# A fused attention and two-mixer kernel: another order for the first 500 steps, and another tile layout and rounding order in the last stage

## The chip, the cores and the metric

The kernel runs on one core of a Trainium2 chip. The metric is the device time of one execution in microseconds. The core has five engines that each run their own instructions in order: TensorE (PE in the profile, with PEld for its weight loads), VectorE (DVE), ScalarE (ACT), GpSimd (POOL) and SyncE (SP), which here only issues DMAs.

## What is computed

Three layers follow one another on 4 batches of 576 rows with 512 channels: attention (a pooled one and one over a band of 7 keys, added), a token mixer and channel mixer, and a second mixer that multiplies by cosine and sine. The weights come as 64-bit floats.

```python
a_d   = sm_attn(mean4(q), mean4(k), mean4(v))        # 8 heads, 144 pooled rows
a_loc = softmax over |i - j| < 4 of q k^T / 8, times v
x = repeat(a_d, 4) + a_loc                            # (4, 576, 512)
u = x + (relu(x^T @ w_tok1) @ w_tok2)^T
x = u + relu(u @ w_ch1) @ w_ch2
theta = x @ w_theta
y = w_tok_r @ (x cos(theta)) + w_tok_i @ (x sin(theta))
u = x + y
out = u + relu(u @ w_ch)
```

## The kernel before

Each matrix product is done with operands split into a rounded part and a rest (`split`, L150: a cast on ScalarE, a subtraction on VectorE), in three matmuls (`mm3`, L155).

**The front.** Everything up to the last stage is written as generators, one for each step; the string ORDER lists in which order they are advanced, one entry for one call (`G3` is one call, `I*2` two). Each call issues the instructions up to the generator's next yield, and every engine then runs what it was issued in exactly that order. Whatever stands first in the list stands first in each engine's queue, and a waiting instruction holds up all that is listed behind it on its engine. The steps of the first 500 entries:

- `P` (16) loads the q and k of a pair of heads (582 KB, 4 buffers); `K` pools them on VectorE (two additions). `W` loads the values of a pair for the band, in 4 DMAs. `V` (8, one for each group of two pairs) loads pooled values (650 KB, one buffer) and adds them on GpSimd in two additions and a product.
- `L` is the band attention of a pair, 8 calls: TensorE starts the scores (with 24 or 12 warming matmuls for the first four pairs, WARM), scores (80 matmuls), VectorE maximum and difference, ScalarE exp, TensorE transposes, ScalarE copies, TensorE output (80 matmuls), VectorE normalization.
- `F` is the pooled attention of a group Q, 9 calls; the seventh normalizes on VectorE, the eighth stores the result (`od`), the ninth waits for that store and loads it back repeated (`xu`). `A` adds `xu` to a pair on VectorE.
- `T` is the token mixer of a group: T.1 casts x on ScalarE, T.2 subtracts on VectorE (`xl`, L606), T.3 copies rows on ScalarE, T.4 and T.5 are the first product on TensorE, T.6 to T.9 the second. `E` evicts and splits the hidden rows, `U` evicts the output (ScalarE twice) and stores it to `uT` from a tile with one buffer.
- `C` is the first part of the channel mixer for 384 columns: C.1 loads from `uT` (so it waits for the stores of `U`), C.2 casts, C.3 subtracts, C.4 to C.11 are TensorE's. `H` and `O` evict.
- `G0` to `G6` and `X` convert 64-bit weights (`converted`): a DMA, a pair of instructions on ScalarE, three on VectorE (L203, L206, L215), one on GpSimd, a cast on ScalarE, a subtraction on VectorE. G0 and G1 are 512 KB, G2 128 KB, G3 to G6 288 KB each, X0 to X7 512 KB each. X28 to X31 are early parts of a late weight; they load through the GpSimd queue (X29 through SP) and write the halves back to memory. X30 is a small one of 64 columns.

A number behind a dot after these names is the call: T2.4 is the fourth call of group 2's T. Steps such as E2.1 carry a dot in their names already; they are told apart by the text.

**The last stage** (from L1333) is ordered by a scheduler, not by hand. For each batch `stage_z` (L1160) makes theta on TensorE in chunks, turns it to cosine and sine, multiplies by x and splits into zh and zl; chunk (4, 1) holds the last 64 rows of two batches, which go to the small tiles eh and el. Batch 0 does this in two halves of 256 columns. `stage_y` (L1202) multiplies by the token weights, reading eh/el first, then zh/zl. The tiles z, uh and ul come from one pool that lies where the front's last tiles were, and a first write to a tile waits until the tile that lay there before has been read.

Of the kernel before, what the change touches and what calls it, by code (L numbers as in the profile page):

```python
# [43 lines left out]
C0 V6 V5 L8 X3 E3.1 L9 H0.3 F5 E3.1 X3 W10 L9 F6 X3 F5 L10 V6 A9 T3 F5 T3 V6 U3.0 L10 K14 T3 V6 U3.0 X6 U3.0 T3 H0.3
X3 X6 X29 X31 X30 X28 L11*2 C0 L11 P15 U3.1*2 A8 F6 U3.1 C0 F5 T4 X29*2 X28*2 X30*2 L11 L12 L10 O0.1 K15 C0 C1 W11 L10
X29 O0.0 X28 C0 T4 X28 T4 F7 O0.3 O0.2 L12 C1 O0.3 T4 L12 F7 L12 T4 C1 L11 E4.1 F6 L11 F7 L11 F6 C1 A10 W12 E4.0 L11
X28 X30*2 X28 X29*3 F6 F7 E4.0 A11 X30*2 F7 X28*3 L12 E4.1 C1 H1.0 T5 C2 F6 L13*2 H1.1 X31 X30 X29 L12 H1.1 T4 T5 T4
U4.0 L13 X30 X29 X30 X29 C1 U4.0 H1.0 U4.0 L13 V7 T4 H1.2 T5 L13 L15 L13 X31*5 T4 U4.1 X31 L12 U4.1 L15 L12 X31 W15 V7
C1 H1.2 A12 V7 U4.1 T5 H1.3 V7 X31 H1.3 L13 E5.0 C1 L13 F7 C1 F7 E5.0 F7 L15 L14*2 A13 L15 C1 O1.0 L14 F7 O1.1 L14 T5
W14 C1 E5.1 C2 E5.1 T6 L14 L15 L14 T5 T6 T5 U5.0 C2 T5 U5.0 L15 U5.0 T5 O1.2 T6 O1.3*2 L15 L14 T6 U5.1 L14 U5.1*2 L15  # L50
T6 E6.0 A14 A15 C2 E6.1 C3 E6.0 T7 E6.1 T6 T7 H2.0 T6 U6.0 H2.0 T7*2 U6.0*2 C3 T6*2 T7 U6.1*2 E7.0 U6.1 C2 E7.1*2 E7.0
T7 H2.1*2 T7 U7.0 T7 U7.0*2 T7 C2*2 H2.2 U7.1 H2.2 U7.1 C3 U7.1 R0 X8 X17 H2.3 X11 H2.3 C2 X19 C2*2 X8 O2.1 X8 C2 O2.2
X8 O2.0 X11 C3 O2.3*2 X21 C3 H3.0 X19 H3.0 X19 X8 C3 X17 X8 X17 C4 H3.1 C3 H3.2*2 X17 H3.1 X19 X20 H3.3 X21 H3.3 C3
X11 X9 C3 C4 O3.0 X21 X17 X19 C3 C4 X21 C3 O3.2 X11 X21 X13 C4 O3.3 O3.1 X21 O3.3 X12 X17 X9 C4 X9 X20 X19 C4 X9 H4.0
X13 H4.0 X20 C5 C4 X15 H4.2 H4.1 X9 H4.1 X20 H4.2 H4.3 B2 X16 H4.3 C4 X9 X13 C4 C5 X13 X20 C4 O4.1 X12 X10 C5 X13 C4
O4.2 X12 B2 C5 O4.0 X12 X11 X13 C5 O4.3 H5.0 X20 X16 O4.3 X23 B2 C5 H5.1 X10 H5.0 X10 C5 H5.2 X12 X11 X10 H5.1 B2 H5.3
X14 X10 H5.3 J2 H5.2 X16 C5 M2.4 X23 X10 X16 X23 X15 C5 X18 C5 O5.1 X23 X22 B2 O5.2 O5.0 X12 X15 X14 C5 X23 X14 X16
M2.5 B2 O5.3 X14 X16 O5.3 R1 X18 X15 X23 X32 X33 M2.4 X34 M2.5 X35 X22 X18 X14 B2 X15 X22 X18 M2.6 B2 X18 X14 X22 M2.7
X15 X18 X22 B2 M2.6 M2.8 X22 M2.7 B2 M2.8 M2.9*2 B2 M2.10*2 B3 M2.11*2 S0 S1 S2 S3 S4 B2 S5 S8 S6 S9 S7 B2 S10 S11 B3
S12 S13 N2.0 S14 B3 S15 B2 S16 S17 S18 S19 S20 N2.1 S21 S22 S23 S24 S25 N2.0 B2 S26 N2.0 S27 S28 N2.2 S29 S30 S31 S32  # L60
N2.1 S33 N2.1 S34 S35 B3 S36 S37 S40 N2.3 S41 S38 S39 B3 M3.4 N2.2 S42 N2.2 S43 S44 B3 S45 S46 N2.3 S47 M3.5 S48 N2.3
S49 S50 B3 M3.6 S51 M3.4 S52 N2.3 S53 M3.5 S54 S55 B3 M3.7 S56 S57 S58 M3.6 M3.7 B3 M3.8 S59 S60 M3.8 S61 S62 J3 S63
B3 M3.9 R3 PL0 X32 M3.9 PL0*2 X33 B3 X32 M3.10 X34 X33 X32 M3.11 X32 M3.10 X33 M3.11 X35 X32 B3 X34 X32 PS0 B3 X33
N3.0 X34 PT0.0 N3.0 PT0.0 PS0 N3.0 X34 B3 PT0.0 PS0 PT0.1 N3.1 PT0.1*2 B3 PT0.3 N3.2 PT0.3 N3.1 PT0.3 N3.1 PT0.2
PP0.0.1 PS0 PT0.2 PP0.1.1 PT0.2 PP0.0.3 N3.3 PH0.0.1 N3.2 PP0.1.3 PH0.1.1 N3.3 N3.2 PP0.0.2 X33 X35 PP0.1.2 PH0.0.2
N3.3 PP0.0.5 PH0.1.2 PH0.0.2 X35 PP0.1.5 N3.3 PH0.0.5 X33 PH0.0.5 PP0.0.6 X35 PH0.1.5 PP0.1.6 PH0.1.5 PH0.0.6 PP0.2.1
PH0.1.6 PH0.0.6 X34 PH0.0.6 X34 X35 X24 PH0.1.2 X35 PP0.3.1 PH0.1.6*2 PP0.0.7 PP0.1.7 PH0.0.7*2 PP0.0.4 PH0.1.7
PH0.0.7 X24 PP0.1.4 PH0.0.4 PP0.2.3 PH0.1.7 PH0.1.4 PH0.0.4 X24 PH0.2.1 PP0.3.3 PH0.3.1 PH0.1.4 PP0.2.2 PH0.1.7 X24
PH0.0.4 PP0.3.2 PH0.2.2 PH0.1.4 X24 PH0.2.2 PP0.2.5 PH0.3.2 PP0.3.5 PH0.2.5*2 PP0.2.6 PH0.3.5 PP0.3.6 PH0.3.5 PH0.2.6
PH0.3.6 PH0.2.6 PP0.2.7 X24 PH0.3.6 PP0.3.7 PH0.2.7 X25 PH0.2.7 PP0.2.4 PH0.3.7 PH0.2.6 PH0.3.7 PP0.3.4 PH0.3.6  # L70
PH0.2.7 J1 PH0.3.7 X27 PH0.3.2 X41 X25 PL1 PH0.2.4 PL1 PH0.3.4 PL1 PH0.2.4 X25 PH0.3.4 D1*2 PH0.2.4 X25 N1.0 PH0.3.4
X25 N1.0 X27 N1.0 X25 X27 X41 D1 X26 N1.1 X27 X41 PS1 X27 N1.1 D1 X41 N1.2 N1.1 PT1.0 X41 N1.2 X27 N1.2 X41 X26 N1.3
X41 PT1.0 X26 PT1.0 X26 D0 N1.3 PT1.1 X26 N1.3 D0 X26 PT1.1 J0 PT1.1 N1.3 PT1.3 PS1 PT1.3 D0 PT1.3 PS1 N0.0 N0.1 N0.0
# [1361 lines left out]
```

## Time and profile before

| | us |
|---|---|
| median of 3 timed runs | 686.59 |
| lowest, highest | 684.61, 690.44 |
| the profiled execution | 681.57 |
| its span, first to last instruction | 679.80 |
| TensorE busy | 655.9 |
| VectorE busy | 521.0 |
| ScalarE busy | 321.2 |
| GpSimd busy | 98.5 |

The busy times are shares of one profiled execution. The time of a step list is best read by stretches: what an engine did between two moments, and what ended its idle time.

### The profile page before, as it was taken

What the parts mean: (1) busy time and instruction counts of PE and PEld (TensorE: products, weight loads), DVE (VectorE), ACT (ScalarE), POOL (GpSimd) and SP (SyncE); (2) the same over time, 40 slices, a digit from 0 to 9 for tenths busy, and PEclk for the clock granted to TensorE, in tenths of its full rate; (3) what the DMA queues carried; (4) which work ended last, traced back from release to release, by engine and by line L of the source; (5) the groups of instructions that cost most, each with busy time, mean ns of one, the idle gap of its engine ahead of it and who ended that gap; (6) DMA issues with size and microseconds to landing.
All of it is one profiled execution on the core that took longest, in us unless ns stands there. A gap on an engine that the chain in (4) does not pass through costs nothing.

```text
span 679.8 us, 17390 instructions
## 1 busy us (share of the span) xinstructions
PE 655.9 (96%) x7320; PEld 626.7 (92%) x7320; DVE 521.0 (77%) x952; ACT 321.2 (47%) x632; POOL 98.5 (14%) x92
## 2 busy tenths in 40 slices
PE   6769899999999999999999999999999999999997
...
GB/s 282 239 277 229 250 274 260 252 179 238 110 157 104 242 293 186 202 62 207 66 194 127 209 142 85 238 324 279 130 63 0 112 114 1 62 141 1 71 1 69
DMA packets 93022, 109.93 MB, mean 162 GB/s; under 512 B 46881, under 2 KB 69537, under 8 KB 92945
## 3 DMA queue, kind: packets, MB, share of 16 engines
...
## 4 chain that ended last, share of the span: by engine, by line
PE 84%; DVE 8%; DMA 3%; ACT 3%; SPq 1%; issue 1%; DVEq 0%; ACTq 0%
PE y L157 6%; PE y L158 6%; PE y L159 6%; PE c L157 4%; PE c L158 4%; PE c L159 4%; PE c L699 4%; PE c L702 4%; PE c L700 4%; PE c_p L905 3%; PE c_p L902 3%; PE c_p L903 3%; PE t L157 2%; PE t L159 2%; PE t L158 2%; DMA qk<-qkT 2%
## 5 line engine op out<-in xcount | busy, mean ns | idle before, releaser
L157 PE MATMUL y<-wrh,zh 128*128 128x288 f32 x256 | 75.0, 296 | 0.8 <-ACT zh L151 0.8
L158 PE MATMUL y<-wrl,zh 128*128 128x288 f32 x256 | 74.9, 296 | 0.0
L159 PE MATMUL y<-wrh,zl 128*128 128x288 f32 x256 | 72.9, 295 | 0.0
L219 POOL TENSOR_TENSOR ww<-ww,raw 128x512 int32<-128x512 int32 (+2 forms) x30 | 41.1, 1373 | 159.2 <-DMA raw<-w_ch 52.5
L157 PEld LDWEIGHTS y<-wrh,zh 128*128 128x128 f32 x256 | 48.0, 188 | 1.1 <-ACT zh L151 1.1
L158 PEld LDWEIGHTS y<-wrl,zh 128*128 128x128 f32 x256 | 48.0, 188 | 0.0
L159 PEld LDWEIGHTS y<-wrh,zl 128*128 128x128 f32 x256 | 47.3, 188 | 0.0
L219 POOL TENSOR_TENSOR raw<-raw 128x512 int32<-128x512 int32 (+2 forms) x16 | 20.0, 1249 | 136.7 <-DVE raw L215 74.1
L1212 DVE TENSOR_TENSOR cx<-y,cx 128x288 f32<-128x288 f32 x32 | 14.4, 455 | 30.3 <-PE y L159 29.9
L151 ACT CAST cuh<-cx 128x288 fp32r<-128x288 f32 (+1 forms) x16 | 8.8, 553 | 57.5 <-DVE cx L1212 57.4
L157 PE MATMUL th<-thh,cxh 128*128 128x512 f32 (+1 forms) x92 | 31.6, 343 | 0.0
L158 PE MATMUL th<-thl,cxh 128*128 128x512 f32 (+1 forms) x92 | 31.6, 343 | 0.0
L159 PE MATMUL th<-thh,cxl 128*128 128x512 f32 (+1 forms) x92 | 31.6, 343 | 0.0
L199 ACT ACTIVATE ww<-raw 128x512 f32<-128x512 f32 (+2 forms) x30 | 19.5, 649 | 25.3 <-DVE c1l L223 9.4
L921 DVE SCALAR_TENSOR_TENSOR g<-c,g 128x384 fp32r<-128x384 f32 x40 | 21.1, 550 | 12.9 <-ACT g L918 12.9
L918 ACT ACTIVATE g<-c 128x384 fp32r<-128x384 f32 x40 | 19.1, 490 | 24.4 <-PE c L159 24.3
L201 ACT ACTIVATE raw<-raw 128x512 int32<-128x512 uint32 (+3 forms) x46 | 29.5, 640 | 0.0
L568 PE MATMUL o<-vw,plt 38*32 38x65 f32 x1280 | 18.0, 236 | 6.9 <-issue 3.6
L929 DVE TENSOR_TENSOR ut<-c,ut 128x384 f32<-128x384 f32 x32 | 17.1, 551 | 9.8 <-PE c L702 9.8
L568 PEld LDWEIGHTS o<-vw,plt 38*32 38x32 f32 x1280 | 15.4, 110 | 9.6 <-issue 4.8
L157 PE MATMUL t<-w2h,h 128*128 128x256 f32 (+1 forms) x64 | 21.6, 337 | 0.0
L157 PE MATMUL c<-uh,c1h 128*128 128x384 f32 x64 | 21.4, 334 | 0.0
...
## 6 DMA issues: line engine op xcount, KB each, us to landing
...
```

The lines of the kernel that those rows point to most:

```text
L157: pe.matmul(out, lh, rh, start=start, stop=False, skip_group_check=again)
L158: pe.matmul(out, lh, rl, start=False, stop=False, skip_group_check=again)
L159: pe.matmul(out, ll, rh, start=False, stop=stop, skip_group_check=again)
L201: act.activation(f, words[:, :, 0], AF.Copy, scale=2.0**-29)
L219: pool.tensor_tensor(out=w.bitcast(I32), in0=w.bitcast(I32), in1=f, op=ALU.add)
L568: pe.matmul(o[r : r + 32, 5 * j + i // 2], pts[h : h + W, i // 2, r : r + 32], vw[h : h + W, g, :], start=True, stop=True,)
L699: pe.matmul(ps[:, 0:MIX], h[:, cb % 2, d], h1, start=cb == cbs[0], stop=False)
L700: pe.matmul(ps[:, 0:MIX], l[:, cb % 2, d], h1, start=False, stop=False)
L702: pe.matmul(ps[:, 0:MIX], weight[cb // 2][2][:, cb % 2, d], h2, start=False, stop=cb == cbs[-1])
L902: pe.matmul(ps[:, 0:MIX], h[:, cb % 2, d], h1, start=cb == cbs[0], stop=False)
L903: pe.matmul(ps[:, 0:MIX], l[:, cb % 2, d], h1, start=False, stop=False)
L921: dve.scalar_tensor_tensor(out=h2, in0=ps, scalar=0.0, in1=h1.bitcast(F32), op0=ALU.max, op1=ALU.subtract)
```

## The change

Two parts. First, the first 500 entries of ORDER are put in another order; they hold the same steps, the same number of times, and from entry 501 on the list is the same. Second, in the last stage the tile uh of batch 0 is allocated ahead of z (so it lies in front of z in the pool), the last rows of a pair's second batch are multiplied and rounded behind the next chunk's casts where the columns come in halves, and ordering edges put the first instructions of later chunks (the scaled copy of theta for the second half, the Abs of a next chunk) behind earlier casts on ScalarE.

```diff
 ORDER = """
-G3 P0 G2 I*2 P1 G3 P4 G3 V0 P2 G3 K0 G3 G2 I G2 I L0*2 P3 K1 F0 W1 L0 F0 L1 L0 G3 F0 V0 L1*2 P5 V0 L2 W0 G2 K2 V0 G2
-F0 G1 L1 V1 F0 L2 K3 G0 G6 K4 L0 F0 L0 L2 L1 G2 F1 L2 K5 L1 L0 F1 G1*2 F1 F0 V1 W3 L0 F1 G5 G0 L1 F0 G0 F1 G6 F2 L1 G0
-P6 W2 G5 G6 L3 V1 F2 F0 V1 L3 G6 F2 F1 L3 G1 G4 F1 L2 P7 L5 L2 K6 L5 F1 G1 L3 A0 V2 X0 A1 L3 G1 T0 L5 G0 T0 L2 G2 F1
-L3 G0 G4 F2 G5 T0*2 V2 X2 L2 G6 W5 F2 K7 V2 L4*2 E0.0*2 T0 L4 V3 V2 A2 L3 E0.1 L5 G4 L4 W4 L5 G6 L5 G4 L3 X2 F3 G5 P8
-P9 A3 G4 F2 G5 E0.1 T1 G4 G5 T0 F2 V3 L4 F3 F2 T0 L4 V3 X2 F3 L6 V3 L6 X7 T0 P11 L6 X2 X0 F3 K8 U0.0 L6 T0 X2 X0 U0.0
-F3 L4 U0.0 V4 K9 F2 F3 X0 L6 L4 L6 T1 F4 U0.1 X0 F3 T1 L5 U0.1 X0 T1 U0.1 F4 X7 X4 V4 F3 T1 X7 F4 W6 L5 X7 E1.1 F4
-E1.0 E1.1 L8 V4 L8 X7 E1.0 X1 A4 F4 T1 P10 A5 T1 X2 T2 L8 T1 U1.0*2 T2 T1 U1.0 X1 F3 L7 X7 L7 T2 X1 T2 X4 X5 K10 X1 L8
...
+P0 K0 G5 I*2 P1 I G1 V0 G6 L1 G4 K1 G1 L0 G3 G5 L1 G5 G1 P2 L0 L1 G2 P4 L0 G6 L0 G4 F0 G6 L2 V0 P3 G2 F0 G5 K2 L2 G2
+F0 L0 L2 V0 G3 F0 K3 L0 V1 X30 V0 F1 P5 G3 G2 G5 F1 W0 F0 V1 L2 L1 G2 L1 G4 K4 G0 L1 G6 F1 F0 X30 V1 W1 L0 P8 G4 G6 G0
+L0 F1 L3 F0 F1 K5 V2 G0 G1 L3*2 L1 G2*2 L1 L2 G1 F0 L2 X2 F0 G0 F2*2 L3 W2 L5 K8 X30 A1 A0 G6 X0 G5 L5 G3 F2 V2 L3 G3
+T0 G0 V1 F1 L5 X30 L3 F2 G4 P11 X0 G1 G3 P6 G0 X30 W3 X2 L4 F1 L4 T0 F2 K6 X0 X4 X2 L2 V2 V3 L2 T0 V2 X0 T0*2 X2 L4 L3
+X0 X2 E0.1 L4*2 P7 K7 W5 F1 L4 E0.0 V3 F2 E0.1 F3 X7 L3 L5 E0.0 L6 F3 F2 T0 G4 L6 F1 W4 L6 X30 P9 T0 F3 X1 U0.0 L5 F3
+L5 T0 V3 F2 X2 X7 L6 A2 U0.0 L4 A3 V4 T1 X7 T0 K9 F3 L6 U0.0 L6 X0 X1 T1 L4 V3 F3 T1 L5 X1*2 I T1 L5 L8 U0.1 E1.0 U0.1
+F2 L8 W6 X1 T1 E1.0 E1.1 F4 L8 L7*2 F3 F4 E1.1 A5 T1*2 U0.1 F4 T1 A4 X7 U1.0 P10 V4 F3 W7 L6 L7 U1.0 F3 U1.0 K10 X7 T1
+T2 L7 X1 L7*2 T2 X3 L8 V4 T2*2 K11 L7 U1.1*2 L6 E2.0 F4 E2.0 A6 F4 X4*3 T2 E2.1 L8 E2.1 L8 L7 P12 T2 A7 L9 X7 F5 U1.1
...
+U3.1 T4 U3.1 C1 X29 L10 L12 K15 C0 F7 X29 T4*2 X29 W11 F7 F5 F7 T4 L10 C0 L12 L13 C1 X29 O0.3 V6 X28 E4.0 O0.2 L12 F6
...
+    def behind(inst):
+        return tc.issue_after(inst.ins) if inst is not None else nullcontext()
...
-            act.activation(t[:, 0:n], ps[:, 0:n], AF.Copy, scale=1.0 / TWO_PI)
+            with behind(first):
+                act.activation(t[:, 0:n], ps[:, 0:n], AF.Copy, scale=1.0 / TWO_PI)
...
-            act.activation(g[:, 0:n], f[:, 0:n], AF.Abs)
+            with behind(first if per == 1 else cast):
+                act.activation(g[:, 0:n], f[:, 0:n], AF.Abs)
...
+                    cast = split(zh[:, i + b0 : i + b0 + nb, d], zl[:, i + b0 : i + b0 + nb, d], wv)
+                if rows:
+                    with behind(cast):
+                        last_rows(1, *rows)
+                    rows = ()
+                if b0 == 0:
+                    zcast = cast
...
+                rows = t[:, 0:width], g, f, xv
+                last_rows(0, *rows)
+                if per == 1:
+                    last_rows(1, *rows)
+                    rows = ()
+        return zcast
...
+    uh = rounded(0)
     z = new_z(0)
-    stage_z(0, 0, 256, *xhl, xx[1], *z)
-    stage_z(0, 256, DM, *xhl, xx[1], *z)
+    zcast = stage_z(0, 0, 256, *xhl, xx[1], *z)
+    stage_z(0, 256, DM, *xhl, xx[1], *z, first=zcast)
```

## Rows read from the trace of the kernel before

**Rows 1.** The page: span, and TensorE's busy tenths in 40 equal slices.

```profile
span 679.8 us, 17390 instructions
...
PE   6769899999999999999999999999999999999997
```

**Rows 2.** Stretches: busy PE, PEld, DVE, ACT, POOL (count); clock, DMA share, GB/s.

```profile
0.00:84.80 84.80, 67.20 (x1881) 54.03 (x1882) 70.67 (x135) 49.08 (x118) 26.81 (x31) 0.92 0.81 255
84.80:154.82 70.02, 68.80 (x1631) 62.24 (x1629) 60.21 (x112) 42.10 (x97) 18.00 (x17) 1.00 0.74 243
154.82:480.53 325.71, 325.65 (x2474) 322.96 (x2467) 243.49 (x436) 145.05 (x270) 53.65 (x44) 1.00 0.59 184
...
0.00:12.70 12.70, 7.95 (x151) 4.96 (x152) 6.47 (x15) 4.01 (x8) 2.57 (x8) 1.00 0.86 307
12.70:46.85 34.15, 24.81 (x856) 19.06 (x853) 28.40 (x55) 19.64 (x50) 9.56 (x10) 0.88 0.82 248
```

**Rows 3.** TensorE in time order: start, us, line, out<-in, shapes, count [idle before <-releaser].

```profile
86.43 0.39 PE L157 MATMUL t<-xh,w1h 128*128 128x256 f32 x1
...
154.82 0.44 PE L629 MATMUL t<-fixed,x 128*128 128x128 f32 x2
...
481.38 0.41 PE L157 MATMUL y<-wrh,zh 128*128 128x288 f32 x1 [0.84 <-ACT zh L151]
```

**Rows 4.** VectorE in order of time, 83 to 95 us.

```profile
83.32 1.48 DVE L606 TENSOR_TENSOR xl<-x,xh 128x1280 fp32r<-128x1280 f32 x1
...
85.57 0.43 DVE L203 TENSOR_SCALAR ww<-ww 128x512 f32<-128x512 f32 x1 [0.17 <-ACT ww L199]
...
89.84 0.56 DVE L546 TENSOR_TENSOR pbuf<-s,mx 128x380 f32<-128x380 f32 x1
...
93.68 0.68 DVE L223 TENSOR_TENSOR c10l<-ww,c10h 128x512 fp32r<-128x512 f32 x1
```

**Rows 5.** VectorE in order of time, 4 to 48 us.

```profile
4.23 0.31 DVE L206 TENSOR_SCALAR raw<-raw 128x288 uint32<-128x288 uint32 x1
...
9.71 0.76 DVE L421 TENSOR_TENSOR qa<-qk 128x576 f32<-128x576 f32 x1 [1.51 <-DMA qk<-qkT]
...
28.10 0.49 DVE L507 TENSOR_TENSOR ods<-od,rd 128x320 f32<-128x320 f32 x1
...
42.15 1.56 DVE L595 TENSOR_TENSOR x<-x,xu 128x640 f32<-128x640 f32 x2 [1.94 <-DMA xu<-ot]
...
47.71 1.33 DVE L206 TENSOR_SCALAR ww<-ww 128x288 uint32<-128x288 uint32 x1
```

**Rows 6.** GpSimd in order of time, 12 to 48 us.

```profile
12.79 1.34 POOL L398 TENSOR_TENSOR vd<-vd 128x650 f32<-128x650 f32 x1 [6.82 <-DMA vd<-vtok]
...
47.46 1.41 POOL L398 TENSOR_TENSOR vd<-vd 128x650 f32<-128x650 f32 x1 [10.48 <-DMA vd<-vtok]
```

**Rows 7.** ScalarE in order of time, three stretches.

```profile
24.05 0.66 ACT L199 ACTIVATE raw<-raw 128x512 f32<-128x512 f32 x1 [0.65 <-DMA raw<-w_tok]
24.61 0.64 ACT L201 ACTIVATE raw<-raw 128x512 int32<-128x512 uint32 x1
...
142.72 1.48 ACT L679 CAST uh<-ut 128x1536 fp32r<-128x1536 f32 x1 [0.47 <-DMA ut<-uT]
...
480.72 0.61 ACT L151 CAST zh<-tg 128x512 fp32r<-128x512 f32 x1
```

**Rows 8.** SyncE's DMA issues in time order: start and length of the issue.

```profile
29.93 0.61 SPq L510 DMA_DIRECT2D od<-ods  x1
...
34.15 0.61 SPq L516 DMA_DIRECT2D xu<-od  x1
...
131.51 0.33 SPq L656 DMA_DIRECT2D uT<-us  x1
...
132.61 1.21 SPq L519 DMA_DIRECT2D xu<-ot  x2
137.37 0.38 SPq L672 DMA_DIRECT2D ut<-uT  x1
```

More of the change, by code (lines that the diff above doesn't have):

```diff
@@ L1 @@
 import math
-from contextlib import ExitStack
+from contextlib import ExitStack, nullcontext
 from functools import partial
@@ L44 @@
[L44 to L73, printed above, removed]
@@ new lines @@
+F2 L8 W6 X1 T1 E1.0 E1.1 F4 L8 L7*2 F3 F4 E1.1 A5 T1*2 U0.1 F4 T1 A4 X7 U1.0 P10 V4 F3 W7 L6 L7 U1.0 F3 U1.0 K10 X7 T1
+T2 L7 X1 L7*2 T2 X3 L8 V4 T2*2 K11 L7 U1.1*2 L6 E2.0 F4 E2.0 A6 F4 X4*3 T2 E2.1 L8 E2.1 L8 L7 P12 T2 A7 L9 X7 F5 U1.1
+L9 X3 L9 V5 U2.0 T2 X3 X29 X4 V4 U2.0 L9 F5 C0*2 F4 X3 F5 P15 C0 W9 L10 T3 X5 T3 L10 V5 T2 W8 T2 U2.0 L9*2 C0 P13 L10
+L8 U2.1*2 X4 L8 H0.0 X5*2 H0.0 L10 L11*2 F4 C0 H0.1 X5 F4 X6 T3 H0.1 T3 L9 E3.0 X28 L11 X3 T3 E3.0 L10 X5 K12 X5 L10
+X6 L9 K13 E3.1 C0 X3 C0 V5 L11 H0.2 F5 X28*2 U2.1 V5 H0.3 X6 E3.1 X6 T3 F5 X28 X30 H0.3 X6 T3 H0.2 X30 V6 U3.0 L11 F6
@@ new lines @@
+P14 F6 T3 V6 L11 X6 U3.0 F5 X28 W10 F4 L12*2 F5 U3.0 A8 A9 F6 C0 T3 V6 F6 K14 X31 F5 L12 C0 O0.0 W12 U3.1 X28 F6 O0.1
+U3.1 T4 U3.1 C1 X29 L10 L12 K15 C0 F7 X29 T4*2 X29 W11 F7 F5 F7 T4 L10 C0 L12 L13 C1 X29 O0.3 V6 X28 E4.0 O0.2 L12 F6
+X28 C1 A10 F6 E4.0 T4 O0.3 L11 C1 L11 X28 F6 A11 C2 C1 H1.1 T5 E4.1 X29 H1.0 H1.1 E4.1 F7 X29 F7 X31 X29 X28 W13 F6
+L13 T4 T5 T4 U4.0 L13 X30 X29 X30 X29 C1 U4.0 H1.0 U4.0 L13 V7 T4 H1.2 T5 L13 L15 L13 X31*5 T4 U4.1 X31 L12 U4.1 L15
+L12 X31 W15 V7 C1 H1.2 A12 V7 U4.1 T5 H1.3 V7 X31 H1.3 L13 E5.0 C1 L13 F7 C1 F7 E5.0 F7 L15 L14*2 A13 L15 C1 O1.0 L14
@@ new lines @@
+PT0.3 N3.1 PT0.2 PP0.0.1 PS0 PT0.2 PP0.1.1 PT0.2 PP0.0.3 N3.3 PH0.0.1 N3.2 PP0.1.3 PH0.1.1 N3.3 N3.2 PP0.0.2 X33 X35
+PP0.1.2 PH0.0.2 N3.3 PP0.0.5 PH0.1.2 PH0.0.2 X35 PP0.1.5 N3.3 PH0.0.5 X33 PH0.0.5 PP0.0.6 X35 PH0.1.5 PP0.1.6 PH0.1.5
+PH0.0.6 PP0.2.1 PH0.1.6 PH0.0.6 X34 PH0.0.6 X34 X35 X24 PH0.1.2 X35 PP0.3.1 PH0.1.6*2 PP0.0.7 PP0.1.7 PH0.0.7*2
+PP0.0.4 PH0.1.7 PH0.0.7 X24 PP0.1.4 PH0.0.4 PP0.2.3 PH0.1.7 PH0.1.4 PH0.0.4 X24 PH0.2.1 PP0.3.3 PH0.3.1 PH0.1.4
+PP0.2.2 PH0.1.7 X24 PH0.0.4 PP0.3.2 PH0.2.2 PH0.1.4 X24 PH0.2.2 PP0.2.5 PH0.3.2 PP0.3.5 PH0.2.5*2 PP0.2.6 PH0.3.5
@@ new lines @@
+PP0.3.6 PH0.3.5 PH0.2.6 PH0.3.6 PH0.2.6 PP0.2.7 X24 PH0.3.6 PP0.3.7 PH0.2.7 X25 PH0.2.7 PP0.2.4 PH0.3.7 PH0.2.6
+PH0.3.7 PP0.3.4 PH0.3.6 PH0.2.7 J1 PH0.3.7 X27 PH0.3.2 X41 X25 PL1 PH0.2.4 PL1 PH0.3.4 PL1 PH0.2.4 X25 PH0.3.4 D1*2
+PH0.2.4 X25 N1.0 PH0.3.4 X25 N1.0 X27 N1.0 X25 X27 X41 D1 X26 N1.1 X27 X41 PS1 X27 N1.1 D1 X41 N1.2 N1.1 PT1.0 X41
+N1.2 X27 N1.2 X41 X26 N1.3 X41 PT1.0 X26 PT1.0 X26 D0 N1.3 PT1.1 X26 N1.3 D0 X26 PT1.1 J0 PT1.1 N1.3 PT1.3 PS1 PT1.3
+D0 PT1.3 PS1 N0.0 N0.1 N0.0 PT1.2 D0 N0.0 N0.2 PT1.2 PS1 N0.1 PT1.2 N0.1 PP1.0.1 N0.3 N0.2 PP1.1.1 PH1.0.1 N0.2
@@ L84 @@
+PH1.3.7 PP1.3.4 PH1.3.6 PH1.2.7 J4 PH1.3.7 PH1.3.2 J5 PH1.2.4 PH1.3.4 PH1.2.4 PH1.3.4 PH1.2.4 D4 PH1.3.4 R5 Z D4 N4.0
+X36 X37 N4.0 LR*2 N4.0 D4 N4.1 X38 LR N4.1 LR D4 N4.2 N4.1 X36*2 X43 X37 X44 N4.3 R6 X36 LR ZS X37 LR X36 N4.2 X37 X38
+ZS D5 N4.2 X36 ZS D5 N5.0 X37 LR ZS LR N5.0 ZS X37 ZS N4.3 ZS D5 N4.3 X43 ZS N5.1 X44 X38 N4.3 LR*2 N5.1 X38 D5 N5.2
+X43 X38*2 X43 X44 X43 N5.3 X44 X43 R6 Z N5.2 X44 N5.3 X44 N5.3*2 LC*2 N5.0 N5.1 N5.2
 """.split()
```

44 lines of the change are left out of this document (26 added, 18 removed).

## Prediction

> **What bounds the kernel now.** I read the page first, then the busy times by stage, then the waits and the order of single instructions on each engine. The page gives a span of 679.8 us and a TensorE that is hardly ever idle after the first slices [rows 1]. The stages make that sharp [rows 2]: in the first 84.80 us TensorE is busy for 67.20 us, so 17.6 us are lost; from 84.80 to 154.82 only 1.22 us are lost; from 154.82 to 480.53 0.06 us; then one gap of 0.84 us [rows 3]. The cut at 84.80 is where VectorE ends T2.2 (83.32 + 1.48) [rows 4]; T2.4, whose second matmul reads that result, starts on TensorE at 86.43, and T4.6, the first step behind the reordered part, at 154.82 [rows 3]. So behind T2.4 there is next to nothing to win, and the front is judged by one question: when does VectorE end T2.2 in the new order? VectorE is busy for 70.67 of the 84.80 us before it [rows 2].
>
> I map steps to rows by counting: every step issues a known number of instructions on each engine, in the order of the list, so the n-th instruction of an engine belongs to a known step.
>
> **The front, part one: VectorE up to T2.2.** The new list holds the same steps, so no instruction is saved. In front of T2.2 it puts everything that the old one had there, and more: X1.3, K10.1, L7.3 (these run from 85.57 to 90.40 in the old order, 4.83 us), X1.6 (0.68) and three small instructions of X30 (64 columns; the 288-column one took 0.31 [rows 5], so 0.6 for the three, 0.9 at most) [rows 4]. Together +6.1 us. What pays for it must be idle time.
>
> Start. The old order feeds VectorE early with G3, the smallest useful weight. The new one loads P0, G5, the constants, P1, G1, V0, and on ScalarE G1's pair of conversions stands in front of G5's, so VectorE, after K0 and K1, waits for G1. When does G1 land? In the old order P1 was there at 9.71 with 1693 KB queued up to it [rows 5], V0 at 12.79 with 2925 KB [rows 6]: 400 KB/us. In the new order 2077 KB are queued up to G1: about 10.7. G1's ScalarE pair costs 0.66 + 0.64 [rows 7] and G5's shorter one about 0.8, so VectorE starts G5.3 at about 12.7, having done only K0 and K1 (2.7 us): 10.0 us idle. The old order had by then 12.70 - 6.47 = 6.2 us idle [rows 2]. Term: +3.8 (between +3.0 and +4.6, by 0.8 us of G1's landing).
>
> Weight conversions beside GpSimd. G5.3 took 2.58 us in the old order, from 47.38 to 49.95; its second instruction took 1.33 where the same one took 0.31 at 4.23 [rows 5], and GpSimd was adding values at 47.46 for 1.41 [rows 6]. G1.3 (2.56, against 1.54 for its shape elsewhere) and G6.3 (2.0 against 1.08) show the same. In the new order these three run early. Free of GpSimd they would save 3.4 us, beside it nothing. V0 lands within a microsecond of them, so GpSimd's additions meet part of them: I take half, -1.7. [...]
>
> Waits between 12.70 and 46.85. VectorE was idle for 34.15 - 28.40 = 5.75 us there [rows 2]: 1.94 for the pooled rows xu [rows 5], the other 3.8 mostly short waits for TensorE. In the new order VectorE runs later against TensorE, so I keep 2.2 of the 3.8 (1.0 to 3.8). The xu trip: F0.7 ended at 28.59 and A0 started at 42.15, 13.6 us later [rows 5], of which SP spent time on other loads: od was issued 1.3 us after F0.7, xu 4.2 us after od, and landed 8.0 us after its issue [rows 8]. In the new order SP is free when F0.7 ends (about 33), so the trip should be some 10 us, and about 8.2 us of VectorE work lies between F0.7 and A1.1: a wait of 1.5 (0 to 5.4). Term: (2.2 + 1.5) - 5.75 = -2.05.
>
> Sum for T2.2: 84.80 + 6.1 + 3.8 - 1.7 - 2.05 = 91.0.
>
> **The front, part two: TensorE behind T2.2.** The TensorE work in front of T2.4 differs by three short steps of opposite sign (L6.7 and L7.5 ahead, F4.4 behind), which I set to nothing. If T2.4 starts later than 86.43, the 1.22 us of idle time behind it can go, so break-even is 86.43 + 1.22 = 87.65. At 91.0 the front costs 3.3 us. TensorE has no slack behind it [rows 2], so this reaches the end in full. C0, the next thing that TensorE needs from others, is not later than that: U1.1 is ready on ScalarE 1.6 us after T2.2, its store and C0's load cost together at most what they cost for C1 (5.9 + 5.4 [rows 7, 8]), the cast and the subtraction 1.5 and 1.8, in sum 16.2 behind T2.2; TensorE's own work from T2.4 to C0.4 is about 16.
>
> The clock: the granted clock averaged 0.88 from 12.70 to 46.85 [rows 2], so a part of that stretch ran at the lower level. I expect the same in the new order and charge nothing, because VectorE is the bound there.
>
> **The last stage.** TensorE waits once, 0.84 us at 481.38, for ScalarE's first rounded z, which ScalarE issues at 480.72 [rows 3, 7] although its input was ready some 5 us earlier. With u's tile in front, z no longer lies on the tile that is still being stored, and the new ordering puts the first casts ahead of the next chunk's Abs. The casts are not new, only earlier: 0.6 us each on a ScalarE that idles between. Deferred are the second batch's last rows, which batch 1 reads a whole stage later. Term: -0.85; bounds -0.85 and +0.5 (the second half's evictions now stand behind a cast, and if that cast waits for its memory, they wait too).
>
> **Sum.** +3.3 - 0.85 = +2.45 us: a profiled span of 682.2 instead of 679.8 (that execution took 681.57, below all three timed runs). Against the median of 686.59 this is 689.0.
>
> **Rivals.** (1) Slower: xu comes late. X2's load (512 KB) is now issued between od and xu; if the trip is the old 13.6 us and that load's 2.0 us (at 261 GB/s over that stretch) on top, A1 waits 7.4 instead of 1.5 us and everything up to T2.2 follows: 694.9. It decides as soon as xu lands behind about 41. For it: xu took 8.0 us from issue to landing. Against it: SP and its queue are emptier at that point. (2) Slower: a wait for a store. In the new list C1's load stands directly behind the store U3.1.3; in the old one SP waited from 133.8 to 137.37 for it, 5.9 us after the store's issue, with other work in between [rows 8]. Behind C1 now stand W11 and F5.9 (xu for A10 and A11), behind these on VectorE and ScalarE A10, A11, T5.1 and E4.1, and T4.6 needs E4.1: 5.9 + 0.4 + 1.7 + 8.0 + about 7 = 23 us from the store to T4.6, while TensorE has 440 matmuls in between, at 42 ns each [rows 2] 18.6 us, and is not yet through the step before. A wait of about 2.5 us: 691.5. (3) The start is better than I think: if the three conversions meet no GpSimd work and the short waits vanish, T2.2 ends at 86.6 to 87 and the front costs nothing or gains 1: 685 to 686.5. [...] (4) Faster by over 1%: T2.2 would have to end near 81.6; VectorE's own work in front of it is 70.67 + 6.1 = 76.8, which leaves 4.8 us of idle time where the start alone costs 10. (5) The last stage does not do what it says and its gap stays: 689.9.
>
> **Chances.** Forecast (T2.2 between 89 and 93, gap gone) 0.45; rival 1 0.13; rival 2 0.15; rival 3 0.20; rival 4 0.04; rival 5 0.03. The three runs shown spread over 684.61 to 690.44, so some 3 us either way come on top. The range reaches from rival 3 with a low run to rival 2 with a high one: 683.0 to 694.5; the likeliest case by itself spans 686 to 691.5. A measurement of this kernel tells about 1% (6.9 us) from no change; slower by more needs rival 1, or rival 2 with a high run: 0.14. Faster by more: 0.06. Same: 0.80.
>
> **What would show it.** Right: VectorE ends T2.2 (the third xl subtraction) near 91 instead of 84.80; its idle time before 12.7 is about 10 us; TensorE's T2.4 starts right behind it and T4.6 near 158; no wait of y for zh. Wrong: T2.2 before 87 (then rival 3), a wait of x for xu longer than 5 us (rival 1), TensorE waiting for h in front of T4.6 (rival 2), or TensorE idle for more than 2 us between 155 and 660.

## The result

| | before | after |
|---|---|---|
| median of 6 timed runs each, us | 684.39 | 692.67 |
| lowest, highest | 681.13, 690.44 | 690.84, 695.47 |
| span of the profiled execution | 679.8 | 691.5 |
| T4.6 starts on TensorE | 154.82 | 167.81 |
| from T4.6 to the end of the span | 524.98 | 523.7 |

The changed kernel is slower: the ratio is 1.0125, with a 95% interval of 1.009 to 1.016. The median of 692.67 lies inside the predicted range of 683.0 to 694.5, but the forecast was 689.0, so the loss was forecast at 2.45 us and is 8.3 us in the medians (11.7 in the two profiled spans). The front loses 13.0 us up to T4.6 (3.3 were forecast), and the stretch behind it gives 1.3 back. That the median lies in the range is luck: the range reached so far up for rival 2 with a high run, and rival 2 did not happen. A loss of over 6.9 us needed rival 1 or 2 in the prediction, which gave it 0.14; neither happened, and it came all the same.

### The profile page after: what moved, and what is told of

Same layout as the page of the kernel before. It is cut to its first block, busy times and chain, and to the rows that moved or that the text cites. A ratio compares the mean times of both kernels' runs of the same rounds, so it can differ in the third digit from the quotient of the medians.

```text
span 691.5 us, 17395 instructions
## 1 busy us (share of the span) xinstructions
PE 662.2 (96%) x7320; PEld 630.6 (91%) x7320; DVE 519.2 (75%) x952; ACT 320.3 (46%) x632; POOL 97.6 (14%) x92
## 4 chain that ended last, share of the span: by engine, by line
PE 89%; DVE 4%; DMA 3%; issue 1%; ACT 1%; SPq 1%; DVEq 0%
PE y L158 6%; PE y L157 6%; PE y L159 6%; PE c L699 4%; PE c L157 4%; PE c L702 4%; PE c L700 4%; PE c L159 4%; PE c L158 4%; PE c_p L905 3%; PE c_p L902 3%; PE c_p L903 3%; PE th L158 2%; PE th L159 2%; PE th L157 2%; PE t L157 2%
## 5 line engine op out<-in xcount | busy, mean ns | idle before, releaser
L921 DVE SCALAR_TENSOR_TENSOR g<-c,g 128x384 fp32r<-128x384 f32 x40 | 21.0, 549 | 17.1 <-ACT g L918 17.1
L929 DVE TENSOR_TENSOR ut<-c,ut 128x384 f32<-128x384 f32 x32 | 17.1, 550 | 10.2 <-PE c L702 10.2
L159 PE MATMUL c<-uh,c1l 128*128 128x384 f32 x64 | 21.4, 334 | 0.0
L158 PE MATMUL c<-ul,c1h 128*128 128x384 f32 x64 | 21.4, 334 | 0.0
```

What stands on the lines that cost most here:

```text
L158: pe.matmul(out, lh, rl, start=False, stop=False, skip_group_check=again)
L159: pe.matmul(out, ll, rh, start=False, stop=stop, skip_group_check=again)
L921: dve.scalar_tensor_tensor(out=h2, in0=ps, scalar=0.0, in1=h1.bitcast(F32), op0=ALU.max, op1=ALU.subtract)
```

## The profile after

First the stretches, which answer [rows 2]: how long, busy time (instructions) of PE, PEld, DVE, ACT and POOL, granted clock, DMA share, GB/s.

```profile
0.00:92.50 92.50, 72.85 (x2031) 57.35 (x2031) 74.22 (x146) 50.19 (x122) 28.81 (x33) 0.89 0.77 249
92.25:167.81 75.56, 70.22 (x1482) 63.04 (x1480) 55.49 (x103) 41.26 (x95) 16.95 (x19) 0.95 0.70 209
...
0.00:11.88 11.88, 8.68 (x200) 5.76 (x200) 2.49 (x5) 3.20 (x6) 1.76 (x7) 1.00 0.86 303
11.88:45.87 33.99, 21.26 (x657) 15.32 (x657) 29.49 (x59) 18.51 (x53) 15.45 (x15) 0.84 0.78 246
14.80:21.60 6.80, 3.84 (x48) 2.56 (x49) 6.51 (x13) 2.47 (x8) 2.41 (x4) 0.50 1.01 371
42.10:52.40 10.30, 8.62 (x197) 6.11 (x184) 8.71 (x19) 7.60 (x19) 1.67 (x2) 0.50 0.90 276
59.20:62.60 3.40, 3.40 (x53) 3.18 (x56) 3.26 (x7) 1.05 (x3) 2.59 (x2) 0.50 0.64 201
117.20:124.00 6.80, 5.17 (x30) 4.97 (x18) 3.08 (x9) 1.70 (x5) 3.26 (x4) 0.50 0.20 58
68.00:92.25 24.25, 23.38 (x665) 20.38 (x666) 21.87 (x43) 16.46 (x39) 4.60 (x4) 1.00 0.70 230
125.30:167.81 42.51, 42.51 (x847) 38.57 (x846) 32.07 (x61) 23.35 (x54) 9.24 (x11) 1.00 0.68 206
```

VectorE ends T2.2 at 92.50 instead of 84.80. Of the 7.7 us, 3.55 are work (74.22 against 70.67) and 4.15 are idle time. But look at TensorE in the row from 68.00 to 92.25: it is busy for 23.38 of 24.25 us. Ahead of T2.4 it doesn't wait for anybody; it arrives late by itself. The four rows with a granted clock of 0.50 are the second thing: TensorE spent 27.3 us at that clock up to T4.6. In the kernel before it spent 13.7 us there, in two spells:

```profile
28.30:35.10 6.80, 5.71 (x141) 3.93 (x134) 6.30 (x14) 2.73 (x7) 2.81 (x4) 0.50 0.79 226
45.30:52.20 6.90, 6.33 (x113) 5.34 (x114) 6.73 (x11) 4.92 (x13) 2.89 (x3) 0.51 0.79 260
```

Next the waits of TensorE up to 170 us, before and then after: line, what was waited for, sum in us, how often, the longest.

```profile
PE o L568 <- issue: 3.6, 2, 2.5
PE o L568 <- DVE pbuf L546: 3.3, 1, 3.3
PE s L533 <- issue: 2.7, 3, 1.5
PE sd L434 <- DVE qkd L422: 1.7, 1, 1.7
...
```

```profile
PE sd L434 <- DVE pbuf L546: 6.3, 1, 6.3
PE s L533 <- issue: 3.8, 4, 1.6
PE o L568 <- issue: 2.3, 2, 2.1
PE t L158 <- issue: 2.2, 1, 2.2
PE o L568 <- DMA vw<-vloc: 1.5, 1, 1.5
...
```

"issue" is time in which TensorE waited for nothing that the profile shows. These rows looked like crumbs when I predicted. The single gaps in the changed kernel, in TensorE's order of time:

```profile
17.76 0.66 PE L434 MATMUL sd<-qkd 64*32 64x144 f32 x9 [6.35 <-DVE pbuf L546]
...
39.95 0.25 PE L568 MATMUL o<-vw,plt 38*32 38x65 f32 x3 [2.07 <-issue]
...
57.77 0.39 PE L158 MATMUL t<-xl,w1h 128*128 128x256 f32 x1 [2.22 <-issue]
...
92.25 0.36 PE L157 MATMUL t<-xh,w1h 128*128 128x256 f32 x1
...
114.99 1.24 PE L568 MATMUL o<-vw,plt 38*32 38x65 f32 x80 [1.53 <-DMA vw<-vloc]
...
118.94 0.28 PE L533 MATMUL s<-qk 64*32 64x38 f32 x2 [1.63 <-issue]
...
119.64 0.52 PE L158 MATMUL c<-ul,c10h 128*128 128x384 f32 x1
...
167.81 0.44 PE L629 MATMUL t<-fixed,x 128*128 128x128 f32 x2
...
493.19 0.30 PE L158 MATMUL y<-wrl,zh 128*128 128x288 f32 x1
```

They answer [rows 3]. T2.4 comes at 92.25 (86.43 before), T4.6 at 167.81. L8.7 waits 1.53 us for the values that W8 loads, and 1.63 us later comes a gap in the middle of L11.2, between two equal matmuls. The matmul of C0.5 behind it takes 0.52 us where the same one in C0.4 took 0.34, at the lower clock. Around 493 the first matmuls that read zh follow one another without the gap of 0.84 us.

Counting TensorE's records (matmuls, weight loads and some 100 of its sequencer) in order gave the surprise. Every gap in front of a matmul that waits for no semaphore (the signal by which one engine releases another) stands at number 193 + 256 n (give or take 3): 7 in this trace, 4 in that of the kernel before, and so in all others of this study. The profile's list of DMA queues has a queue for instructions:

```profile
q8 instruction: 57, 0.93, 0.6%
```

That is 57 packets of 16 KB each, about one for 256 of TensorE's 14,749 records. In the raw trace such a packet ends 1.0 to 1.7 us ahead of the end of each such gap (for the gap that ends at 118.94 it ran from 116.50 to 117.59). I call these gaps stops at a block boundary.

## The experiments

Three theories went in. A: TensorE's own idle time, and the lower clock that follows it, cost the front as much as VectorE's work, above all at F0.1 and at L8.7. B, that of the prediction: everything follows from VectorE's end of T2.2. C, formed after the first four runs and an assumption of mine from the packets above: TensorE can't run faster than its instructions come, so idle time taken away in one place comes back at the next block boundary.

All numbers below are from one profile of each run, and the ratio to the kernel before from the timed runs. "Stops" and "waits" are TensorE's idle time up to T4.6 at block boundaries and for other engines, "clock 0.50" is how long the granted clock was 0.50 up to T4.6.

| run | T4.6 | stops | waits | clock 0.50 | ratio, 95% interval |
|---|---|---|---|---|---|
| before | 154.8 | 5.2 | 12.4 | 13.7 | |
| last_only | 157.2 | 5.1 | 13.2 | 13.7 | 0.997, 0.9936 to 1.0004 |
| pad128_before | 160.5 | 7.8 | 9.4 | 20.5 | 1.0052, 1.003 to 1.0075 |
| pad60_before | 168.6 | 10.3 | 12.1 | 27.3 | 1.028, 1.0256 to 1.0305 |
| after | 167.8 | 8.4 | 15.4 | 27.3 | 1.0125, 1.009 to 1.016 |
| front_only | 169.9 | 8.8 | 15.4 | 27.3 | 1.0108, 1.0048 to 1.0168 |
| w8_early | 167.5 | 11.7 | 10.6 | 20.5 | 1.0108, 1.0062 to 1.0154 |
| l1_first | 169.6 | 13.6 | 9.2 | 23.9 | 1.0118, 1.0069 to 1.0168 |
| pad106_after | 166.2 | 9.1 | 11.0 | 13.7 | 1.0122, 1.01 to 1.0143 |
| pad106_moved | 167.7 | 10.7 | 12.8 | 17.1 | 1.0124, 1.0077 to 1.017 |
| warm8 | 170.0 | 6.4 | 20.8 | 30.7 | 1.0113, 1.0077 to 1.0149 |
| lean_dve | 172.6 | 9.2 | 14.7 | 30.7 | 1.0201, 1.0156 to 1.0247 |
| apart | 166.7 | 9.1 | 13.2 | 27.3 | 1.0122, 1.0087 to 1.0157 |
| pad106_gap | 167.9 | 9.4 | 12.2 | 23.9 | 1.0157, 1.0112 to 1.0202 |

One thing has to be known before the columns are compared. front_only has the same list as the changed kernel, and w8_early and apart have it up to a point behind T2.4. Yet T2.4 starts at 92.25 in the changed kernel and, in these three in this order, at

```profile
94.72 0.36 PE L157 MATMUL t<-xh,w1h 128*128 128x256 f32 x1
...
95.14 0.36 PE L157 MATMUL t<-xh,w1h 128*128 128x256 f32 x1
...
93.49 0.36 PE L157 MATMUL t<-xh,w1h 128*128 128x256 f32 x1
```

The stops ahead of it, in the changed kernel and in these three, are 5.9, 7.2, 8.7 and 7.4 us. So one profile of the same instructions differs from the next by up to 2.9 us there. A part of it arises at the start, where the same 24 warming matmuls took 3.42 us in the changed kernel and in apart, 4.89 in front_only and 5.29 in w8_early. Behind T2.4 the profiles agree better: from there to T4.6 it is 75.56 us in the changed kernel and 75.20 in front_only (68.39 before, 69.89 in last_only).

**Which part loses: front_only, last_only.** The first takes the new list with the old last stage, the second the old list with the new last stage.

> The new list with the old last stage. Theory: the whole loss lies in the front. In the profile of the changed kernel T4.6 starts 13.0 us later than before (167.81 against 154.82), and the last stage gives about 0.9 us of it back. So this kernel should be about 9 us slower than before in the timed runs (0.85 slower than the changed kernel's +8.3), T4.6 near 168, and TensorE should wait 0.8 us for the first rounded z. Rival: the new last stage costs something that the profile hides; then this kernel is faster than the changed one, +6 us or less.

> The old list with the new last stage. Theory: the gap of 0.84 us ahead of y's first use of zh is gone and nothing else changes: 0.85 us faster than before, the same within the spread. T4.6 stays at 154.8. Rival: the casts moved ahead delay the evictions behind them, and the gap comes back elsewhere: 0 to 0.5 us slower.

Both came out as the first theory said. front_only is 1.08% slower and waits in the last stage as the old kernel did:

```profile
496.53 0.40 PE L157 MATMUL y<-wrh,zh 128*128 128x288 f32 x1 [0.85 <-ACT zh L151]
```

last_only doesn't wait there. Its stretch behind T4.6 is 0.6 us shorter than before, and its median 683.2 against 685.08; the interval reaches just over 1, so a gain of this size stays unproven in time. The whole loss lies in the list.

The diffs of the list below show only the pieces of its lines where something is put in or changes place.

**Two waits taken away: w8_early, l1_first.**

```diff
-F5 C0*2 F4 X3 F5 P15 C0 W9 L10 T3 X5 T3 L10 V5 T2 W8 T2 U2.0
+F5 C0 W9 W8 C0 F4 X3 F5 P15 C0 L10 T3 X5 T3 L10 V5 T2*2 U2.0
```

> The changed kernel, with the loads W9 and W8 issued directly behind C0.1 instead of 7 and 15 entries later; nothing else moves. In the changed kernel L8.7 waits 1.53 us for W8's values, TensorE's instructions then stop once more for 1.63 us (L11.2), and the granted clock falls to 0.72 and 0.60 from 115 to 125. Theory A (a late load in front of a step of TensorE decides here, and its idle time brings the lower clock): wait gone, clock 1.0 through C0.5, which took 4.21 us and should take 2.3; T4.6 starts 4 to 6 us earlier (162 to 164), the time is 4 to 6 us shorter than the changed kernel's. Rival B (everything behind T2.2 follows from VectorE's end of T2.2 at 92.5): what is saved at L8.7 is waited for at the next hand-over from VectorE, and T4.6 moves by less than 1.5 us.

```diff
-G3 G5 L1 G5 G1 P2 L0 L1 G2 P4 L0 G6
+G3 G5 L1 P2 L0 L1 G2 P4 L0 G5 G1 G6
```

> The changed kernel, with VectorE's part of the weight conversions G5.3 and G1.3 moved behind the maximum and difference of the first two pairs (L1.3, L0.3). In the changed kernel F0.1 waits 6.35 us, to 17.76, for L1.3, which stands behind both conversions; and the granted clock is 0.50 from 15 to 20. Theory A (TensorE's idle time and the clock that falls with it cost the front as much as VectorE's work): F0.1 starts at 12 to 13, clock 1.0 to 20, VectorE 1.2 us less idle ahead of 12; T2.4 on TensorE 3 to 5 us earlier (87 to 89), time 3 to 5 us shorter. Rival B (VectorE's sum of work ahead of T2.2 decides, and TensorE has time to spare in this stretch): only the 1.2 us of VectorE's idle time are won; T2.2 ends at 91.3.

Both did what they were built for, in their place. With the early loads L8.7 starts without a wait and the granted clock is 1.00 from 110 to 130, through C0.5 (C0.4 to T3.4: 8.6 us, after 12.1):

```profile
116.59 0.33 PE L159 MATMUL c<-uh,c10l 128*128 128x384 f32 x1
116.86 1.22 PE L568 MATMUL o<-vw,plt 38*32 38x65 f32 x80
118.01 0.34 PE L530 MATMUL s<-fixed,id 128*128 128x190 bf16 x2
118.28 0.89 PE L533 MATMUL s<-qk 64*32 64x38 f32 x78
120.81 0.23 PE L533 MATMUL s<-qk 64*32 64x38 f32 x2 [1.65 <-issue]
```

In l1_first VectorE is done with both pairs at 15.1, and F0.1 starts at 14.22. But it comes only as far as the block boundary:

```profile
14.22 0.48 PE L434 MATMUL sd<-qkd 64*32 64x144 f32 x16 [0.70 <-DVE pbuf L546]
...
18.65 0.72 PE L434 MATMUL sd<-qkd 64*32 64x144 f32 x13 [3.54 <-issue]
```

So the 6.35 us at F0.1 had two causes that end within a microsecond of each other (17.76 in the changed kernel, 18.65 here): VectorE's conversions, and a stop at a block boundary. In both runs the waits fell (15.4 to 10.6 and 9.2 us), the stops rose (8.4 to 11.7 and 13.6), and no change of the time is clear of the intervals. For w8_early most of this is not the edit: its stops and waits differ ahead of T2.4, where nothing was moved. Behind T2.4 its gain stays: T2.4 to T4.6 takes 72.40 us, 2.8 to 3.2 less than in the two profiles without the edit. T4.6 comes at 167.54 all the same, because T2.4 came at 95.14. Theory A's sizes (3 to 6 us) were too large; rival B's reason was wrong too, since in l1_first the time went into stops and in w8_early what was saved was not waited for at a later hand-over.

**Instruction supply: pad60_before, pad128_before.** The list of the kernel before, untouched, with small matmuls at TensorE's start (here 60; their result is overwritten, so nothing of the computation changes):

```diff
         warm(s[:, 0, 192:512], WARM[n])
+        for _ in range(60 if n == 0 else 0):
+            pe.matmul(s[0:32, 0, 192:230], zero[0:64, 0:32], zero[0:64, 0:38], start=True, stop=True)
```

> The kernel before, its lists untouched, with 60 small matmuls (38 columns, result unused) on TensorE behind the first pair's warming matmuls, where TensorE then waits 1.5 us for a constant anyway. With its weight load each is two instructions, so every later instruction of TensorE has a number that is 120 higher. Theory C (instruction supply): in every trace so far each gap of TensorE that no wait explains stands at instruction 193 + 256 n, a 16 KB load of the instruction queue ends about 1.4 us ahead of its end, and a block of 256 instructions never took less than 3.45 us. Which block a dense step falls into then decides. The sum over the blocks of what their own work lacks to 3.9 us is 25.5 us for the old list, and 34.9 us for the same list shifted by 120: 5 to 9 us slower than before, with boundary stalls of 9 us or more in place of 5.2. Rivals (VectorE's work decides, or the waits as listed): the list is the same, so at most the matmuls' own time, 0 to 1 us slower.

> The same with 128 small matmuls: 256 instructions, so the blocks of the old list lie as they did before, one block later. Theory C: no slower than what these matmuls cost at the start, 0 to 2 us, and clearly faster than the one with 60. If it is matmuls at the start that cost (a later start, a changed clock), it is slower than the one with 60, by twice as much over the kernel before.

This is the decisive pair. Sixty extra matmuls cost 19 us, 128 cost 4. With the 128, TensorE was busy with warming and small matmuls 5.1 us longer (16.5 us, 11.4 before), with the 60 1.1 us longer. What differs is the place of the boundaries: with 60 there are 16.4 us of stops over the whole run (three of them, 2.94, 2.93 and 3.14 us, behind 150 us, where the kernel before has none), with 128 there are 7.8. And this stop cost more than its length:

```profile
106.50 0.33 PE L158 MATMUL c<-ul,c10h 128*128 128x384 f32 x1
108.92 0.44 PE L159 MATMUL c<-uh,c10l 128*128 128x384 f32 x1 [2.08 <-issue]
109.20 0.34 PE L157 MATMUL c<-uh,c10h 128*128 128x384 f32 x1
...
110.41 0.53 PE L157 MATMUL c<-uh,c10h 128*128 128x384 f32 x1
```

Behind the 2.08 us of the stop the matmuls of one chain go from 0.34 to 0.53 us, and the stretch reads 0.50:

```profile
110.10:113.50 3.40, 3.40 (x12) 3.40 (x11) 1.83 (x2) 0.83 (x2) 0.00 (x0) 0.50 0.83 285
154.40:157.90 3.50, 3.50 (x19) 3.50 (x19) 1.39 (x1) 0.00 (x0) 0.00 (x0) 0.51 0.16 55
```

Stops and lower clock together account for nearly all of the profile of pad60_before, which is 23.8 us longer than that of the kernel before: its stops are 11.1 us more; 1.1 are the small matmuls; and TensorE was busy for 34.9 us in stretches at a clock of 0.50 (12.0 before). Half of these 22.9 us is 11.5; by the pace of one chain in the changed kernel, whose matmuls follow each other at 0.18 us in C0.4 and at 0.32 in C0.5 at the lower clock, it is 10.2. The kernel before has the same list and the same waits (12.1 and 12.4 us). So another place of the boundaries alone cost this kernel more than the change did (19 us against 8.3). Theory C's sum said 9.4 us for the 60; it had no term for the clock that falls.

**The same on the new list: pad106_after, pad106_moved, warm8, pad106_gap.** 106 such matmuls in the pair L1; with both moves of above; WARM = [8] instead of [24] for the first pair; and the 106 in front of F0.1.

> The changed kernel with 106 such matmuls in its first pair: 212 instructions. Theory C: by the same sum the new list lacks 34.4 us as it stands and about 28.7 us shifted by 212, so 3 to 6 us faster than the changed kernel (686 to 689 where before is 685). Rivals: order and waits are the same, so the time is that of the changed kernel or up to 2 us longer.

> The same 106 matmuls together with both moves that gave nothing alone (W9 and W8 directly behind C0.1; VectorE's G5.3 and G1.3 behind L0.3). Theory C: each of the moves took a wait away (waits 15.4 to 10.6 and 9.2 us), and the stall at the block boundaries rose by as much (8.4 to 11.7 and 13.6 us); with another place of the boundaries part of what the moves save should stay, so faster than the one with 106 matmuls alone, by 1 to 4 us. If the moves are simply worth nothing (VectorE decides), it is the same as that one.

> The changed kernel with 8 instead of 24 warming matmuls in the step L0.1, so 32 instructions fewer on TensorE ahead of everything. Theory C (instruction supply): the blocks of 256 shift, and the sum of what each block's own work lacks to 4.0 us falls by 2.7 to 4.1 us (34.2 to 31.9, or 27.6 to 23.6, by how a matmul's own time is taken); with some 2 us less of warming, T4.6 starts 3 to 6 us earlier than in the two profiles of this list (167.8 and 169.9). Rival D (the clock needs these matmuls): the lower clock comes once more or earlier, a spell of it is 3.4 us or longer and costs half of its length: same time or up to 3 us slower.

> The changed kernel with the 106 small matmuls not at the start, where they took 5.6 us, but in front of F0.1, where TensorE waited 3.5 to 6.3 us in the profiles of this list. From there on its blocks lie as in the run with 106 at the start. Theory C (instruction supply and the clock that falls with it): at the start those 106 took 3.7 us of gaps and 5.4 us of lower clock away and cost 5.6 us themselves. Here they should cost 0 to 3 us, since they fill a wait: T4.6 at 160 to 165 instead of 167.8 and 169.9, and 3 to 7 us shorter than the changed kernel, 686 to 690 where before is 685. Rival E (the gaps of this list are what its other waits leave, and move wherever room is made): T4.6 within 2 us of 168, and the time that of the changed kernel.

All four missed theory C's gain: the first three have the changed kernel's ratio (1.0122, 1.0124 and 1.0113 against 1.0125), and that of pad106_gap is higher (1.0157), with an interval that overlaps. In pad106_after the lower clock went back to 13.7 us and the idle time from 23.8 to 20.0, but warming and small matmuls took 5.7 us longer (17.1 us against 11.4) and T4.6 moved by only 1.6. Behind T2.4 the shift did what theory C said: L11.2 runs without a stop, and T2.4 to T4.6 takes 70.99 us in pad106_after and 71.65 in pad106_gap, where W8 is as late as in the changed kernel (75.56). Ahead of T2.4 it was lost again: T2.4 starts at 95.18 and 96.28. warm8 lost in waits (20.8 us; 7.0 of them at F0.1, again for VectorE) what its stops saved (6.4). pad106_gap shows most plainly why filling this wait with matmuls didn't work:

```profile
12.01 0.70 PE L433 MATMUL pad<-zero 64*32 64x38 bf16 x22
18.03 1.04 PE L433 MATMUL pad<-zero 64*32 64x38 bf16 x28 [5.32 <-issue]
```

The added matmuls themselves ran into the boundary and waited 5.32 us there. In the raw trace the packet ahead of it ran from 15.21 to 16.55, 4.1 us behind the moment when TensorE entered the block before it.

**VectorE's part: lean_dve.** K10.1, X1.3 and three small instructions of X30 go from in front of T2.2 to behind it, X1's last three calls behind L6.8.

```diff
-T2 X3 L8 V4 T2*2 K11 L7 U1.1*2 L6 E2.0
+T2 K10 X1 X30*3 X3 L8 V4 T2*2 K11 L7 U1.1*2 L6 X1*3 E2.0
```

> The changed kernel with K10.1, X1.3 and the three small instructions of X30 moved from in front of T2.2 to directly behind it (and X1's last steps behind L6.8): VectorE has 3.9 us less to do ahead of T2.2, as in the old list. Theory of the prediction (the end of T2.2 on VectorE decides, TensorE follows): T2.2 ends at 88.5 instead of 92.5, T4.6 starts 3 to 4 us earlier, and the time is 3 to 4 us shorter. Theory C (TensorE's own losses decide; T2.2 only ends at about the time at which TensorE arrives): T2.2 may end earlier, but T2.4 still starts directly behind L7.5, above 91, and T4.6 moves by less than 1.5 us.

VectorE had 70.65 us of work up to the end of T2.2 in place of 74.22, and ended it at 93.37, not at 88.5; the list as it was ended it between 92.50 and 95.42 in four profiles. It now waits in front of it:

```profile
91.88 1.49 DVE L606 TENSOR_TENSOR xl<-x,xh 128x1280 fp32r<-128x1280 f32 x1 [1.70 <-ACT xh L603]
```

T2.4 starts at 93.01 directly behind L7.5, as theory C said. T4.6 didn't stay, though: the moved work now stands ahead of L6.8 on VectorE, F4.4 waits 3.51 us for that, the granted clock is 0.50 from 98.3 to 105.2, and the ratio is 1.0201. VectorE's work has little room on either side of T2.2.

**Two dense steps apart: apart.** The early loads, and in addition C0.5 between L8.7 and L11.2.

```diff
-L8 H0.0 X5*2 H0.0 L10 L11*2 F4 C0 H0.1
+L8 H0.0 X5*2 H0.0 L10 F4 C0 L11*2 H0.1
```

> The changed kernel with the early W9 and W8 (directly behind C0.1) and with L11.1 and L11.2 behind C0.5 instead of in front of it, so that the 80 small matmuls of L8.7 and the 80 of L11.2 have the 12 large ones of C0.5 between them. In every run of the new list so far, also the one with the early loads, TensorE stopped for 1.63 to 1.65 us in L11.2, where a block of 256 lasted 3.45 to 3.52 us. Theory C: with 2.2 us of other work in between that stop is gone (under 0.2 us), no spell of the lower clock stands between 110 and 130, and the stretch from C0.4 to T3.4 is 1.5 us shorter than with the early loads alone; time 1 to 3 us shorter than the changed kernel's. Rival: the stop is a wait that the profile does not show, and stays with the step: 1.6 us in L11.2 wherever it stands.

In its place it did what was expected: L11.2 takes 0.91 us without a stop, and C0.4 to T3.4 is 6.6 us, 2.0 less than with the early loads alone (8.6; 12.1 after). One sign failed: a spell of the lower clock (0.50) stands from 111.0 to 114.4, behind another stop; none follows in the front.

```profile
118.11 0.44 PE L157 MATMUL c<-uh,c10h 128*128 128x384 f32 x1
...
120.60 0.91 PE L533 MATMUL s<-qk 64*32 64x38 f32 x80
121.44 0.38 PE L157 MATMUL t<-xh,w1h 128*128 128x256 f32 x1
```

The rival, a hidden wait of the step itself, is out. But two stops of this run, 2.03 us at 78.60 and 1.74 at 109.97, are longer than those of the changed kernel nearby (0.21 and 0.77), the first of them at a place that the edit doesn't touch. T2.4 to T4.6 takes 73.25 us, 2.3 less than in the changed kernel, and T4.6 is 1.1 us earlier. The timed runs, whose interval is 0.35% (2.4 us) to either side, can't show that.

## Why the prediction was right and wrong

- **VectorE up to T2.2: nearly right.** Forecast 91.0, with 89 to 93 as the likely case; measured 92.50, but 93.98 to 95.42 in the three other profiles of the same instructions, so the nearness is in part luck. The work that now stands ahead of T2.2 came to some 5.1 us (3.55 more work, and the 1.5 saved at the conversions; forecast 6.1). The start cost 3.2 us more idle time than before (9.4 up to 11.88, against 6.2; forecast 3.8). The three conversions took 5.6 us where they had taken 7.1 (a saving of 1.5; forecast 1.7). The waits from there to A1 fell by 1.25 (forecast 2.05), and xu was waited for not at all. Not forecast were 2.2 us more idle time between 46 us and T2.2.
- **"VectorE is the bound": wrong.** This is the step that failed. T2.4 comes directly behind L7.5, TensorE is busy for 23.38 of the last 24.25 us, and lean_dve took 3.6 us of work from VectorE without T2.2 getting earlier than the list as it was had it. The prediction's own sign, T4.6 near 158, failed with it (167.81). From "VectorE is busy for 70.67 of 84.80 us" I concluded that it decides; but TensorE was then losing 17.6 us of its own, 4.4 of them at boundaries where it waited for no engine, and the prediction has no term for those rows.
- **"The clock: charge nothing": wrong.** Up to T4.6 TensorE was busy for 136.0 us before (67.20 + 68.80, [rows 2]) and is for 142.8 now, 6.8 us more for the same matmuls. In the spells at a clock of 0.50 it was busy for 12.0 us before and is for 21.0 now; of these 9.0 us, by my estimate 4.0 to 4.5 are what the lower clock costs (from the 0.18 against 0.32 us of one chain, or half, from the 0.50). The other 2.3 to 2.8 us I can't place. Idle time rose by 6.2 us (18.8 to 25.0): 3.0 for waits, 3.1 for stops.
- **"Behind T2.4 nothing but its own work": wrong.** T2.4 is 5.8 us late and T4.6 is 13.0. In the part between I had checked C0 only. C0 was indeed no later than TensorE. What I overlooked stands on SyncE: W8 was moved to 8 entries ahead of L8.7, 37 before, and SyncE issued its parts from 106.72 to 111.71, so L8.7 waited 1.53 us; the stop in L11.2 and 6.8 us at the lower clock followed. From C0.4 to T3.4 w8_early and apart take 3.5 and 5.5 us less; in the timed runs this doesn't show. Smaller: E2.1's second instruction stands behind X4.3 on VectorE, and TensorE waits 0.56 us for it.
- **Rivals.** (1), xu late, did not happen: VectorE reached A1 at 45.87 and xu was there. (2), the store wait of C1, did not happen: TensorE is busy for 42.51 of 42.51 us ahead of T4.6. (3) and (4) would have needed a T2.2 before 87. (5), the gap that stays, did not happen.
- **The last stage: right.** The gap is gone, alone and together with the list; behind T4.6 the kernel is 0.6 (last_only) to 1.3 us shorter, forecast 0.85.

What stays open is why the new list is slower by 1.1 to 2.0% in every shape that I gave it. Behind T2.4 the 7.2 us lost are mostly traced (the late W8, the stop, the spell), and edits took back 2.3 to 4.6 of them there. Ahead of T2.4 idle time moved between waits and stops, no edit brought T2.4 below 92.25, and a single profile is too uncertain (up to 2.9 us) to say more. The old list loses 2.8% at the one other place of its boundaries that was run (a shift of 120; the shift of 256 puts them back), so part of the loss may be a lucky fit given up and not the new order as such. One other place doesn't settle this; the new list was run at three places (shifts of 0, of 212 and of 32 the other way) and lost 1.1 to 1.3% at each.
